# One inverse round earlier, one half round later: moving the scratch loads and the last jobs of a tiled convolution

## The chip, the cores and the metric

The kernel runs on one core of one Trainium2 chip. The metric is the device time of one execution in microseconds (us). Besides the plain timed runs there is one execution taken with the hardware profiler; all durations below are from it.

## The reference

The reference convolves an image of 224 x 224 pixels with 96 channels in and 96 out with a 7 x 7 filter, cyclically, by way of Fourier transforms in both directions:

```python
wp = jnp.pad(w, ((0, H - K), (0, W - K), (0, 0), (0, 0)))
Xf = rfft2(x, axes=(1, 2)); Wf = rfft2(wp, axes=(0, 1))
Yf = jnp.einsum('bhwi,hwio->bhwo', Xf, Wf)
y = irfft2(Yf, s=(H, W), axes=(1, 2)).astype(jnp.bfloat16)
```

x is 1 x 224 x 224 x 96 and w is 7 x 7 x 96 x 96, both bfloat16. Any method that gives this cyclic convolution will do.

## The kernel before

The kernel transforms the height only. The 224 rows are cut into 8 blocks of 28 (`B`, `NJ`), and each block with its 6 rows of overlap becomes 34 real numbers, held as 17 frequencies (`NS`) with a real and an imaginary part. Along the width the 7 taps stay a direct convolution, with adjacent pixels taken in pairs so that three short convolutions do the work of four. The image is cut into 7 tiles of 32 columns (`NT`, `TL` is the last, number 6). Every tile goes through three stages.

- Forward (`a_jobs`, `f_jobs`): TensorE multiplies the pixels `xn` by the transform matrix `Fm`; ScalarE (ACT) or VectorE (DVE) copies the result from PSUM to `xf`.
- Rounds (`b_round`, L496): one round for each frequency `s` = 0 to 16. First DVE forms sums and differences `J` of neighbouring pixels for three frequencies at once (`jit`, L466). In a round TensorE fills a first PSUM bank (19 small matmuls with `J`, `xf` and the filter `WF`); ACT scales part of it (`tt_`) and DVE makes `u` from it; then the function `mid` is called; TensorE fills a second bank (14 matmuls); DVE makes `v`; GpSimd (POOL) or DVE adds both to `yf`; at the end the function `end` is called. After three frequencies `yf` is stored to a scratch tensor `scr` in DRAM (`put`, L590). In the last tile this store is put off to the next round and queued on ACT's own instruction stream (L593 and L557); its scratch tensors are called `scra` and `scrb`.
- Inverse (`c_jobs`, L645): the scratch is read back with frequencies on the partitions (`load_t`, L602, tiles `tt` and `tt2`), TensorE multiplies by the inverse matrix `Gm`, ACT or DVE copies the result to `yo` (or to a free part of `J2`, which profiles call J), and it is stored to `out_dram`. A tile has 11 such jobs of two matmuls each: 2 + 2 + 3 + 2 + 2 for the five loads of `LT` (L685). The third load is `tt2`, made of four DMAs.

The stages of different tiles are interleaved, and the order is written out by hand in the loop from L808. While tile t is in its rounds, TensorE also gets the forward jobs of tile t+1 and the inverse jobs of tiles t-2 and t-1. They are dealt out by half round (`pace`, L725): a half round 2s is the `mid` of round s, 2s+1 its `end`. `CQ` (L42) says how many inverse jobs of the older and of the newer tile run during tile t: (11, 3) in tile 3, (8, 7) in tile 4, (4, 11) in tile 5 and (0, 11) in tile 6. They are spread evenly over the half rounds `k0` to `k1`, the older ones first (L819 to L826).

Loads of the scratch are queued by `queue_c` (L695) at the start of round 3. It hands the five loads to `pump` (L690), which issues a load as soon as fewer than four `tt` tiles (one for `tt2`) are held; a job that finishes a tile calls `pump` again. All loads, all stores of tiles before the last, and all output stores are issued by one queue, SyncE (SP), strictly in order: an entry whose semaphore is not there yet holds all entries behind it. Each DMA also takes one of eight semaphores in turn and waits until the DMA that had it before has landed.

PSUM has eight banks, given out in turn (`bank`, L106). A matmul that starts a new bank waits until the engine that reads the bank's former content is done. The program's builder fixes which bank, and therefore which reader, that is.

After the last round come the loads of the last scratch (`load_b`, L620), eight matmuls on the part that is already there (`first`), 36 matmuls that only keep TensorE working (L866), and sixteen closing matmuls (`second`) with their copies and stores.

Of the kernel before, what the change touches and what calls it, by code (L numbers as in the profile page):

```python
# [17 lines left out]
NS = L // 2  # L18
# [38 lines left out]
def kernel(  # L57
# [10 lines left out]
    TL = NT - 1  # L68
# [65 lines left out]
    def dma(out_ap, in_ap):  # L134
        return DE.dma_start(out=out_ap, in_=in_ap)
# [298 lines left out]
    def a_jobs(t):  # L434
        xf = new_xf(t)
        jobs = []
        for jg in range(2):
            for h in range(2):
                for (q, n) in ((0, 3), (3, 3), (6, 2)):
                    jobs.extend(a_bank(t, xf, xn_bufs[jg], h * PXC + 2 * q, n, jg, HALO + h * 8 + q))  # L440
            jobs.append(then_load(jobs.pop(), t + 1, jg))
        return jobs
# [23 lines left out]
    def jit(t, g):  # L466
        s0, s1 = JGB[g]
        n = s1 - s0
        xf = xf_tiles[t][0:C]
        xv = xf.rearrange("c p r s w j -> c p r s (w j)")  # L470
        b = jcount[0] % 3 if t < 2 else (jcount[0] - 2 * len(JGB)) % 2
        jcount[0] += 1
        Jb = J_bufs[b][0:C].rearrange("c (k s q) -> c k s q", k=7, s=3)
        for s in range(s0, s1):
            jbuf[(t, s)] = Jb[:, :, s - s0]

        def sub(o, a, b, op, cost):
            def f():
                load["v"] += 170 + cost / 1.92
                return VE.tensor_tensor(out=o, in0=a, in1=b, op=op)  # L480
            return f
        x0, x1 = xv[:, 0, :, s0:s1], xv[:, 1, :, s0:s1]
        c0, c1 = max(s0, REAL[0] + 1), min(s1, REAL[1])
        i0, i1 = c0 - s0, c1 - s0
        pd, rd, sd, qd = x1.ap
        dpl = bass.AP(x1.tensor, x1.offset - NJ, [pd, [NJ, 2], rd, sd, qd])
        return [
            sub(Jb[:, 0:4, 0:n].rearrange("c (k r) s q -> c k r s q", r=2), dpl,
                x0.unsqueeze(1).to_broadcast([C, 2, 2, n, PP]), ALU.subtract, 4 * PP * n),
            sub(Jb[:, 4, i0:i1], xv[:, 0, 0, c0:c1], xv[:, 0, 1, c0:c1], ALU.add, PP * (c1 - c0)),  # L490
            sub(Jb[:, 5:7, i0:i1], Jb[:, 0:4:2, i0:i1], Jb[:, 1:4:2, i0:i1], ALU.add, 2 * PP * (c1 - c0)),
        ]
# [152 lines left out]
    def c_jobs(t):  # L645
        jobs = []
        w0 = t * 2 * TW
        for gi, h in LT:
            hold = {}
            nq = 2 if gi < 2 else 3  # L650

            def mk_(q, gi=gi, h=h, nq=nq, hold=hold):
                def put(j0, nj, px, npx, row, col):
                    dma(out[0, j0 * B:(j0 + nj) * B, w0 + px:w0 + px + npx, :].rearrange("h w c -> h (w c)"),
                        hold["yo"][row:row + nj * B, col:col + npx * C])

                def f():
                    if q % 2 == 0:
                        hold["yo"] = new_yo()
                    tt = tt_tiles[(t, gi, h)]  # L660
                    yo = hold["yo"]
                    nj = 2 if q == 2 else 3
                    for b in range(2):
                        pb = bank()[0:nj * B, 0:4 * C]
                        TE.matmul(pb, lhsT=G[0:nj * FR, 0:nj * B],
                                  rhs=tt[0:nj * FR, 4 * q + 2 * b:4 * q + 2 * b + 2, :].rearrange("p w e -> p (w e)"), start=True, stop=True)
                        k = 2 * (q % 2) + b
                        evac(yo[0:nj * B, k * 4 * C:(k + 1) * 4 * C], pb, 4 * C)
                    if q == 1 and gi < 2:
                        put(gi * 3, 3, h * PXC, PXC, 0, 0)  # L670
                    elif q == 1:
                        put(6, 2, 0, 16, 0, 0)
                        for j in range(2):
                            put(6 + j, 1, 24, 8, 2 * B, j * 8 * C)
                    elif q == 2:
                        put(6, 2, 16, 8, 0, 0)
                    if q == nq - 1:
                        held[gi == 2] -= 1
                        pump()
                return f  # L680
            for q in range(nq):
                jobs.append(mk_(q))
        return jobs
# [11 lines left out]
    def queue_c(t):  # L695
        pend.extend((t, *k) for k in LT)
        pump()
# [35 lines left out]
    def fills(qs, k):  # L733
        def f():
            for q in qs:
                pace(q, k)
        return f
# [3 lines left out]
    def add(a, b, jobs):  # L741
        qs.append([a, b, jobs, len(jobs)])
# [15 lines left out]
    for r in range(NS + LAG):  # L758
# [32 lines left out]
        for t in range(2):  # L791
            s = r - LAG * t
# [15 lines left out]
    for t in range(2, NT):  # L808
        if t == TL:
            scr_tiles[t] = None  # L810
            scr_tiles[(t, 0)] = dr_pool.tile([TW, NJ, SA, 4 * C], BF16, name="scra")
            for i in range(2):
                scr_tiles[(t, 1 + i)] = dr_pool.tile([TW, NJ, (SB - SA, NS - SB)[i], 4 * C], BF16, name=f"scrb{i}")
        else:
            scr_tiles[t] = dr_pool.tile([TW, NJ, NS, 4 * C], BF16, name="scr")
        qs = []
        if t + 1 < NT:
            add(4 if t == 2 else 0, 26, a_jobs(t + 1))
        nold, nnew = CQ[t]  # L819
        k1 = 2 * NS if t < TL else 2 * NS - 9  # L820
        k0 = 10 if t in (2, TL) else 3
        km = k0 + -(-(k1 - k0) * nold // (nold + nnew))
        add(k0, km, cj[:nold])
        cn = c_jobs(t - 1)
        cj = cn[nnew:]
        add(km, k1, cn[:nnew])  # L826
        plan = {}
        for g, (s0, s1) in enumerate(JGB):
            if g + 1 < len(JGB) or t + 1 < NT:
                plan[s0 if g + 1 < len(JGB) else s0 - 1] = g  # L830
        for s in range(NS):
            now = ()
            if s in plan:
                g = plan[s]
                now = jit(t, g + 1) if g + 1 < len(JGB) else jit(t + 1, 0)
            if s == 3:
                queue_c(t - 1)
            if t in (3, 4):
                next(gp, None)
            if t == TL and s == SA + 2:  # L840
                sv = scr_tiles[(TL, 0)].rearrange("w j s (r e) -> (j s r) w e", r=2)
                for g in range(2):
                    for p0, p1 in ((0, 64), (64, KA)):
                        dma(tl_a[g][p0:p1], sv[g * KA + p0:g * KA + p1])
            b_round(t, s, fills(qs, 2 * s), fills(qs, 2 * s + 1), bool(now) or (t == TL and s >= NS - 3), now)
# [66 lines left out]
```

## Time and profile before

| | |
|---|---|
| median of 3 timed runs | 270.45 us (270.08 to 270.87) |
| profiled execution, its own time | 270.74 us |
| span of the program in it | 269.0 us |
| TensorE (PE) busy | 257.9 us, 96% of the span |
| DVE busy | 214.3 us, 80% |
| ACT busy | 195.5 us, 73% |
| POOL busy | 99.4 us, 37% |
| rounds of tile 5 | about 192 to 224 us |
| rounds of tile 6 | about 224 to 253 us |

A line of the timeline has the start in us from the start of the span, the duration in us, engine, line, operation, output<-inputs with buffer numbers left out, shape and count; in brackets stands how long the engine idled before and what ended that. All instructions bear the line 89, because a helper issues them, so they are told apart by tile names. `SPq` and `ACTq` are the instruction queues that issue DMAs. A matmul's duration contains its latency: successive matmuls overlap, and the time a group takes on TensorE is read from its start to the start of the next group.

### The profile page before, as it was taken

To read this page: it belongs to the slowest core of one execution; us is meant where nothing else is said; L and a number is where in the kernel's file an instruction comes from. 1 tells how busy PE (TensorE), PEld (TensorE's weight loads), DVE (VectorE), ACT (ScalarE), POOL (GpSimd) and SP (SyncE) were. 2 spreads that over 40 slices of the span, in tenths; PEclk is the share of its full clock that TensorE was granted. 3 is DMA by queue.
4 is the path that set the end of the run, shared out by engine and by line. 5 is a ranking of instruction groups with operands and counts; after the bars stand their busy time and mean duration, and the time that the engine had idled before them with its cause. 6 is when DMAs were issued, how large, how long until landed. Compare 5 with 4: busy or idle time off the path is not lost.

```text
span 269.0 us, 12171 instructions
## 1 busy us (share of the span) xinstructions
PE 257.9 (96%) x5144; PEld 237.1 (88%) x5144; DVE 214.3 (80%) x457; ACT 195.5 (73%) x483; POOL 99.4 (37%) x156
## 2 busy tenths in 40 slices
PE   8899999999999999999999999999998999899993
PEld 3679999999998999999999998989997989779862
DVE  5649998889899788778787888777887889778724
ACT  5549988587974578988988789886986864467113
POOL 7782315363647435322322222234132242522100
PEclk9999999999999999999999999999999999999998
DMA  6948011811111597987976486989658834888866
GB/s 171 230 129 217 6 46 46 243 47 67 46 46 50 163 276 135 294 249 206 289 207 198 133 246 192 250 223 332 224 151 152 255 98 154 198 231 212 223 118 205
DMA packets 47014, 46.78 MB, mean 174 GB/s; under 512 B 35286, under 2 KB 37986, under 8 KB 46960
## 3 DMA queue, kind: packets, MB, share of 16 engines
q1 hardware_dynamic: 44672, 43.94, 59.2%
q10 hardware_dynamic: 2288, 2.06, 2.8%
q8 instruction: 40, 0.66, 1.1%
q14 instruction: 14, 0.11, 0.1%
HBM read 24.65 MB, written 21.33 MB: 171 GB/s over the span
## 4 chain that ended last, share of the span: by engine, by line
PE 64%; DMA 12%; DVE 11%; ACT 7%; issue 3%; SPq 2%; DVEq 0%; ACTq 0%
PE pb L89 64%; DMA tt<-scr 5%; DMA wq<-in_w_dram 5%; DVE J L89 4%; ACT WF L89 3%; ACT xf L89 2%; DVE v L89 2%; DVE WF L89 2%; SPq L89 2%; DMA xf<-scrb 2%; DVE u L89 1%; DMA scrb<-yf 1%; DVE yf L89 1%; DVE xf L89 0%; DVE tt L89 0%
## 5 line engine op out<-in xcount | busy, mean ns | idle before, releaser
L89 PE MATMUL pb<-WF,J 96*128 96x96 bf16 x2821 | 162.6, 206 | 1.1 <-DVE J L89 0.9
L89 PEld LDWEIGHTS <-J 96*128 96x128 bf16 x2821 | 138.0, 98 | 10.5 <-issue 2.2
L89 POOL TENSOR_TENSOR yf<-v,u 128x384 bf16<-128x384 f32 x79 | 81.4, 1042 | 147.3 <-issue 86.9
L89 ACT CAST xf<-pb 96x408 bf16<-96x408 f32 (+3 forms) x145 | 67.8, 490 | 8.9 <-PE pb L89 5.3
L89 PE MATMUL pb<-WF,xf 96*128 96x96 bf16 x952 | 59.9, 206 | 0.5 <-ACT xf L89 0.5
L89 DVE TENSOR_TENSOR J<-xf 96x1824 bf16<-96x1824 bf16 (+1 forms) x84 | 56.9, 716 | 0.1
L89 PEld LDWEIGHTS <-xf 96*128 96x128 bf16 x952 | 47.0, 98 | 0.7 <-ACT xf L89 0.6
L89 PE MATMUL pb<-Fm,xn 118*128 118x136 bf16 (+3 forms) x640 | 45.5, 199 | 0.2 <-DVE u L89 0.2
L89 PE MATMUL pb<-tt,Gm 102*84 102x384 bf16 (+1 forms) x132 | 32.7, 327 | 2.4 <-DMA tt<-scr 2.3
L89 ACT CAST WF<-pb 96x480 bf16<-96x480 f32 (+1 forms) x59 | 29.1, 577 | 5.3 <-PE pb L89 5.3
L89 PEld LDWEIGHTS <-xn 118*128 118x128 bf16 x640 | 30.3, 97 | 0.3 <-issue 0.3
L89 ACT CAST J<-pb 84x384 bf16<-84x384 f32 (+1 forms) x64 | 27.6, 488 | 2.3 <-PE pb L89 2.0
L89 ACT CAST yo<-pb 84x384 bf16<-84x384 f32 (+1 forms) x63 | 26.9, 482 | 2.7 <-PE pb L89 2.7
L89 DVE TENSOR_TENSOR J<-J 96x912 bf16<-96x912 bf16 (+2 forms) x42 | 24.2, 576 | 0.0
L89 PE MATMUL pb<-wq 98*128 98x120 bf16 (+1 forms) x288 | 21.3, 226 | 0.3 <-DMA wq<-in_w_dram 0.3
L89 PEld LDWEIGHTS <-wq 98*128 98x128 bf16 x288 | 19.5, 151 | 0.8 <-issue 0.8
L89 PE MATMUL pb<-wu 128*128 128x512 bf16 (+1 forms) x75 | 16.5, 382 | 1.1 <-DVE ct L89 1.1
L89 PEld LDWEIGHTS <-wu 128*128 128x128 bf16 (+1 forms) x75 | 8.8, 119 | 7.7 <-issue 2.4
L89 DVE TENSOR_TENSOR yf<-v,u 128x384 bf16<-128x384 f32 x26 | 14.9, 571 | 0.9
L89 PEld LDWEIGHTS <-Gm 102*84 102x84 bf16 (+1 forms) x132 | 11.0, 117 | 3.5 <-DMA tt<-scr 2.9
L89 ACT COPY xf<-xf 96x816 bf16<-96x816 bf16 (+3 forms) x20 | 11.3, 632 | 0.0
L89 DVE CAST WF<-pb 96x480 bf16<-96x480 f32 (+1 forms) x13 | 7.5, 611 | 4.7 <-PE pb L89 4.7
(386 smaller groups left out, 234.4 us busy)
## 6 DMA issues: line engine op xcount, KB each, us to landing
scr<-yf SPq DMA_DIRECT2D x30, 288.0 KB
xn<-in_x_dram SPq DMA_DIRECT2D x12, 672.0 KB
tt<-scr SPq DMA_DIRECT2D x24, 336.0 KB
out_dram<-yo SPq DMA_DIRECT2D x12, 252.0 KB
out_dram<-J SPq DMA_DIRECT2D x12, 252.0 KB
tt<-scr SPq DMA_DIRECT2D x6, 288.0 KB
WF<-in_x_dram SPq DMA_DIRECT2D x2, 672.0 KB
out_dram<-tt SPq DMA_DIRECT2D x8, 168.0 KB
```

The lines of the kernel that those rows point to most:

```text
L89: r = fn(*a, **k)
```

## The change

Two expressions change. In tiles 3, 4 and 5 `queue_c` is called at the start of round 2 instead of round 3; tiles 2 and 6 keep round 3. In the last tile the inverse jobs are spread over the half rounds from 12 on up to, and not including, 26, where it was from 10 up to 25.

```diff
@@ -817,8 +817,8 @@
         if t + 1 < NT:
             add(4 if t == 2 else 0, 26, a_jobs(t + 1))
         nold, nnew = CQ[t]
-        k1 = 2 * NS if t < TL else 2 * NS - 9
-        k0 = 10 if t in (2, TL) else 3
+        k1 = 2 * NS if t < TL else 2 * NS - 8
+        k0 = {2: 10, TL: 12}.get(t, 3)
         km = k0 + -(-(k1 - k0) * nold // (nold + nnew))
         add(k0, km, cj[:nold])
         cn = c_jobs(t - 1)
@@ -833,7 +833,7 @@
             if s in plan:
                 g = plan[s]
                 now = jit(t, g + 1) if g + 1 < len(JGB) else jit(t + 1, 0)
-            if s == 3:
+            if s == (3 if t in (2, TL) else 2):
                 queue_c(t - 1)
             if t in (3, 4):
                 next(gp, None)
```

In SP's stream this moves, in tile 3, one load ahead of the store of `yf` of rounds 0 to 2; in tile 4, two loads ahead of that store and of one small copy; in tile 5, two `tt` loads and the four DMAs of `tt2` ahead of an output store and of that `yf` store, and a third `tt` load ahead of the `yf` store. In tile 6 the four loads `xf<-scra` for the closing stage come ahead of one output store that stood before them. No instruction is added or dropped; the numbers of matmuls, copies and DMAs stay. Which job lies in which half round of tile 6 changes as follows (jobs 1 to 11 of tile 5's inverse):

| half round | 10 | 11 | 12 | 13 | 14 | 15 | 16 | 17 | 18 | 19 | 20 | 21 | 22 | 23 | 24 |
|---|---|---|---|---|---|---|---|---|---|---|---|---|---|---|---|
| before | 1 | 2 | 3 | - | 4 | 5 | 6 | - | 7 | 8 | 9 | - | 10 | 11 | - |
| after | - | - | 1 | 2 | 3 | 4 | - | 5 | 6 | 7 | 8 | - | 9 | 10 | 11 |

## The prediction

> **What bounds the kernel now.** I read the page first, then PE's waits, then the timelines of PE, SP, DVE and ACT where those waits lie, and the chain of waits at the end.
>
> ```profile
> span 269.0 us, 12171 instructions
> PE 257.9 (96%) x5144; PEld 237.1 (88%) x5144; DVE 214.3 (80%) x457; ACT 195.5 (73%) x483; POOL 99.4 (37%) x156
> ```
>
> PE is the bound, so only what lets PE stand still can be won. PE's waits over the whole span:
>
> ```profile
> PE pb L89 <- DMA tt<-scr: 2.3, 3, 1.1
> ```
>
> Three waits for scratch loads are the largest entry. The PE timeline shows where they are, and the end of the kernel:
>
> ```profile
> 200.58 0.46 PE L89 MATMUL pb<-WF,J 96*128 96x96 bf16 x7
> 200.88 0.28 PE L89 MATMUL pb<-Fm,xn 118*128 118x136 bf16 x2
> ...
> 202.22 0.46 PE L89 MATMUL pb<-WF,J 96*128 96x96 bf16 x7
> 203.79 0.52 PE L89 MATMUL pb<-tt,Gm 102*84 102x384 bf16 x2 [1.10 <-DMA tt<-scr]
> ...
> 230.78 0.46 PE L89 MATMUL pb<-WF,J 96*128 96x96 bf16 x7
> 232.21 0.52 PE L89 MATMUL pb<-tt,Gm 102*84 102x384 bf16 x2 [0.96 <-DMA tt<-scr]
> ...
> 237.99 0.46 PE L89 MATMUL pb<-WF,J 96*128 96x96 bf16 x7
> 238.73 0.52 PE L89 MATMUL pb<-tt,Gm 102*84 102x384 bf16 x2 [0.28 <-DMA tt<-scr]
> ...
> 253.34 0.90 PE L89 MATMUL pb<-xf,GA 72*112 72x384 bf16 x4 [0.23 <-DMA xf<-scra]
> 254.08 6.01 PE L89 MATMUL pb<-wu 128*112 128x384 bf16 x36
> 260.48 0.99 PE L89 MATMUL pb<-xf,GB 128*112 128x384 bf16 x5 [0.39 <-DMA xf<-scrb]
> ```
>
> Seven `J` matmuls take 0.30 us from start to start where work follows at once (200.58 to 200.88). So the job at 203.79 was ready for PE at 202.52: PE lost 1.27 us, more than the idle time printed. By the same working it lost 1.13 at 232.21 and 0.44 at 238.73; before the job at 237.12 (14 matmuls from 236.35, 0.60) another 0.17. In all 3.0 us: 1.27 in tile 5, 1.74 in tile 6. SP's timeline has the loads:
>
> ```profile
> 192.31 0.35 SPq L89 DMA_DIRECT2D scr<-yf  x1
> ...
> 197.76 0.35 SPq L89 DMA_DIRECT2D scr<-yf  x1
> 198.20 7.90 SPq L89 DMA_DIRECT2D tt<-scr  x7
> ...
> 228.41 8.14 SPq L89 DMA_DIRECT2D tt<-scr  x8
> ...
> 245.06 3.44 SPq L89 DMA_DIRECT2D xf<-scra  x4
> ```
>
> **Part 1: the loads a round sooner.** Tile 5 first. The loads need tile 4's last store, issued at 192.31; the chain has 2.39 us from issue to landing for such a store (`scrb<-yf`, 253.89), so they may start at about 195 instead of 198.20. The chain's longest landing of a first tile is 5.54 us (198.20), which gives 200.5, two us before PE wants it: the 1.27 goes. What they are moved past: the J store (issued 196.91) and the `yf` store (197.76) now stand behind six load issues, which took 4.9 us at 228.41 and 6.1 at 198.20, so both come out 4 to 5 us later. Their buffers are wanted again four stores on (about 209) and four groups on (round 12, about 216); no cost, and if that cover were gone, up to 5 us of waiting for ACT or POOL. In tiles 3 and 4 PE never waits for `tt`; first use of the moved loads is ten or more half rounds off, and the one store and small copy behind them have the same cover. Cost nothing.
>
> What is late next: in the changed kernel's streams the banks fall differently from round 11 of tile 5 on. The second bank of that round is now the one that round 10's `u` gives back; before, its reader was a copy on ACT. `u` starts at 214.62 and takes 0.35 on DVE; PE starts the second bank at 214.49. Both come 1.27 earlier, so the wait is 0.48 us. Bounds: 0 if DVE catches up (it idles 0.94 before 210.62, but on ACT's scaled copy, which follows PE), 0.6 if `v` next to it counts too. I take 0.48, the row itself. Tile 5 nets 1.27 - 0.48 = 0.79.
>
> **Part 2: the last tile's jobs.** All loads and landings of tile 6 move with tile 5's end, so I keep the clock of before and add the 0.79 at the end. The second half of round 5 now follows its first at 231.08; PE reaches round 6 at 231.68. The rows that matter:
>
> ```profile
> 230.60 1.40 DVE L89 TENSOR_TENSOR J<-xf 96x1824 bf16<-96x1824 bf16 x2
> 231.93 0.62 DVE L89 TENSOR_TENSOR J<-J 96x912 bf16<-96x912 bf16 x1
> ...
> 247.59 0.54 DVE L89 SCALAR_TENSOR_TENSOR v<-tt__7338,pb 128x384 f32<-128x384 f32 x1
> ```
>
> ```profile
> 235.39 0.33 ACTq L89 DMA_DIRECT2D scra<-yf  x1
> ```
>
> (a) `J` of rounds 6 to 8 is done at 232.00 and 232.55. Round 6's first bank takes 4 matmuls from 232.00, 8 on `xf`, the last 7 from 232.56: it ends at 232.86 instead of 232.49, a new wait of 0.37 (0 if DVE runs ahead, 0.87 if all 19 wait for the last sum). Job 1 is due at 232.86, its tile landed by 232.21; jobs 5 and 6 are due at 238.45 and 239.59 by counting on (0.81 a first bank, 0.60 a second, 0.33 a job, and the waits below), their pieces landed by 237.1 and 238.7. So all 1.74 of load waits go.
>
> (b) ACT works in order. Before, the copies of jobs 1 and 2 ran at 232.60 to 234.38, ahead of the `scra` store that ACT issues at 235.39 once POOL has summed round 5 (233.41 plus 1.96). Now that store stands ahead of them, and POOL's sum hangs on DVE, not PE. ACT is held from 233.4 to 235.82 (its first copy after the store); the four copies then end at 236.30, 236.67, 237.04 and 237.41 (0.37 from start to start). Job 4 reuses job 1's banks: due 235.86, its matmuls start at 236.30 and 236.67; round 8 needs the third copy, 237.04 against 236.83. Wait 0.44 + 0.21 + 0.21 = 0.86. Bounds: 0 if POOL is done in time; 2.0 if the whole hold reaches PE.
>
> (c) The same at the second such store (before, at 241.54, after a hold of about 0.5): jobs 6 and 7 are copied behind it. 0 to 0.5; I take 0.26, the middle.
>
> (d) In round 12 DVE's `v` began at 247.59 though PE's second bank ended at 247.16 and `v` may start 0.19 later (239.88 against 239.69): ACT and `u` came last. With job 11 now between the two banks they have time: a gain of 0.24 for DVE's run of work to the last `yf` (253.87).
>
> Sum for that last `yf`: 0.79 + 1.74 - 0.37 - 0.86 - 0.26 + 0.24 = 1.28 us earlier.
>
> **The tail.** Two things must follow. PE's 36 filler matmuls (6.01 us) start only when the `xf<-scra` loads are in (253.34), and PE waited just 0.39 for `scrb` after them: if these loads keep their time, the end gains 0.39 at most. They should come sooner, as the output store of job 9 (issued 244.64, 252 KB) no longer precedes them. In exchange that store and job 11's now both stand in SP's queue right before the last `scrb` store. At 198.20 the first load took 5.54 us behind two stores (540 KB), at 228.41, with none before it, 3.8: 1.7 us for 540 KB, or 0.8 for the 252 KB that are new. They are issued over a us before the `scrb` store, so part drains in time: cost 0 to 0.8, I take 0.3.
>
> So 1.28 - 0.3 = 1.0 us. The profiled execution took 270.74 (span 269.0), 0.29 over the median; against it the forecast is 269.74, against the median 270.45 - 1.0 = **269.45**. A measurement of this kernel can tell about 0.3%, 0.81 us.
>
> **The rivals.**
>
> - The last store is caught in the queue. If the 504 KB still block it when it is issued, its landing comes 0.8 to 1.7 later; taking 0.9, the end gains 0.4: **270.05**. For it: the row of 198.20. Against it: the two stores may leave a us or more earlier. The Trainium skill (DMA: Bandwidth & Descriptors, Queues, rings and completion order) says that each DMA engine takes the descriptors of one issuing engine's queue in ring order; the 5.54 against 3.8 us agrees, and by that rule alone this rival would be the case.
> - The `scra` loads keep their time, and the fillers hold the end: gain 0.39, **270.06**. For it: SP still has the stores of jobs 5 to 7 before them, and these jobs run a half round later; against it: the fourth load waited for job 9's store at 247.22 and no longer has to.
> - Slower: the `scra` loads come later. Job 7 is a half round (1.0 us) later and its copy is behind (b) and (c); with the full 2.0 of (b) the loads go out 2.2 us later (1.0 + 2.0 - 0.79), and the end comes 2.2 - 0.39 = 1.8 later: **272.25**. It decides from loads 1.2 us late (0.39 + 0.81). Against it: job 7's store had 1.7 us to spare in front of the loads (243.36 to 245.06).
> - None of the new waits appears: 3.0 + 0.24 less nothing, about **267.3**. Against it: DVE is busy almost without a break from 216.8 to 228.8.
>
> **How the numbers follow.** Forecast 0.50 (268.9 to 269.9, of it 0.07 above 269.64), queue 0.18, fillers 0.14, slower 0.12, no new waits 0.06. Faster: 0.43 + 0.06, rounded 0.50; same: 0.07 + 0.18 + 0.14, 0.38; slower 0.12. The range, **268.2 to 270.8**, leaves out the slower rival and the last (0.18): its low end is the forecast with half the new waits (0.98 of 1.97) and no queue cost (0.3), its top the queue rival with 1.7 instead of 0.9.
>
> **What would show it.** Part 1: `tt<-scr` in tile 5 issued near 195, no PE wait near 202.5, but one of about half a us at DVE's `u` near 213. Part 2: no PE wait for `tt<-scr` at all, a wait for `J` at round 6, ACT's copies of jobs 1 and 2 behind the `scra` store, PE waits on ACT copies in rounds 7 to 8. Tail: `xf<-scra` in by about 252, `yf` done near 252.6. I am wrong if a `tt` wait stays, if ACT's hold costs PE over 2 us, or if the `scrb` chain after the last `yf` is longer than its 6.6 us of before (253.87 to 260.48) by more than 0.8.

## The result

The changed kernel takes 269.73 us in the median (269.23 to 270.67, 22 runs), the kernel before 270.56 us beside it (269.39 to 271.69, 22 runs). The ratio is 0.9974, 95% interval [0.9963, 0.9986]: 0.8 us, 0.3%, faster. A second set, told below, had 0.9999 [0.9976, 1.0023]. Weighted by the inverse squares of their widths the two give 0.998, some 0.6 us: a gain, near the least that can be told.

The profiled execution took 269.54 us (270.74 before), its span is 267.8 us. First the engines' busy time on its page, which is that of before:

```profile
span 267.8 us, 12172 instructions
PE 258.4 (96%) x5144; PEld 237.3 (89%) x5144; DVE 214.3 (80%) x457; ACT 194.6 (73%) x483; POOL 98.9 (37%) x156
```

PE's timeline of the changed kernel at the places that the prediction named (start, duration, in brackets the idle time before and what ended it):

```profile
202.02 0.46 PE L89 MATMUL pb<-WF,J 96*128 96x96 bf16 x7
202.32 0.49 PE L89 MATMUL pb<-tt,Gm 102*84 102x384 bf16 x2
...
213.53 0.76 PE L89 MATMUL pb<-WF,J 96*128 96x96 bf16 x14 [0.38 <-DVE u L89]
...
231.10 0.34 PE L89 MATMUL pb<-WF,J 96*128 96x96 bf16 x4 [0.23 <-DVE J L89]
...
235.42 0.70 PE L89 MATMUL pb<-tt,Gm 102*84 102x384 bf16 x2 [0.31 <-ACT J L89]
236.18 0.33 PE L89 MATMUL pb<-WF,J 96*128 96x96 bf16 x4
...
251.01 1.74 PE L89 MATMUL pb<-xf,GA 72*112 72x384 bf16 x8
252.59 6.01 PE L89 MATMUL pb<-wu 128*112 128x384 bf16 x36
259.33 0.97 PE L89 MATMUL pb<-xf,GB 128*112 128x384 bf16 x5 [0.72 <-DMA xf<-scrb]
```

At 202.32 the inverse job follows the seven `J` matmuls after 0.30 us: the 1.27 us that PE lost there are gone. No wait for `tt` is left in either tile. In their place stand the waits for `u` (213.53; the two matmuls before it started at 212.66, and such a pair takes 0.33 from start to start, so the whole loss is 0.54 us, over the 0.38 shown), for `J` (231.10) and for ACT's copies (235.42, and the 0.76 us to the next group instead of 0.33). SP's and ACT's timelines show why, and the chain of waits shows the end:

```profile
192.10 0.35 SPq L89 DMA_DIRECT2D scr<-yf  x1
195.55 4.59 SPq L89 DMA_DIRECT2D tt<-scr  x6
200.25 2.18 SPq L89 DMA_DIRECT2D out_dram<-J  x1
...
243.55 2.67 SPq L89 DMA_DIRECT2D xf<-scra  x4
249.30 0.34 SPq L89 DMA_DIRECT2D out_dram<-J  x1
251.59 0.34 SPq L89 DMA_DIRECT2D out_dram<-yo  x1
252.40 0.35 SPq L89 DMA_DIRECT2D scrb<-yf  x1
```

```profile
234.44 0.33 ACTq L89 DMA_DIRECT2D scra<-yf  x1
234.89 1.61 ACT L89 CAST J<-pb 84x384 bf16<-84x384 f32 x4 [2.05 <-PE pb L89]
```

```profile
252.40 3.73 DMA scrb<-yf
...
256.15 3.13 DMA xf<-scrb
```

The loads of tile 5 start at 195.55 instead of 198.20. In tile 6 ACT stands 2.05 us with its four copies behind the store at 234.44. The releaser named is PE, but PE made these jobs' matmuls at 231.96 and 232.88; the store ahead of them in ACT's own stream is what held them. At the end the store of the last `yf` takes 3.73 us (2.39 before) and its load 3.13 (4.05 before).

### The profile page after: what moved, and what is told of

Same layout as the page of the kernel before. It is cut to its first block, busy times and chain, and to the rows that moved or that the text cites. A ratio compares the mean times of both kernels' runs of the same rounds, so it can differ in the third digit from the quotient of the medians.

```text
span 267.8 us, 12172 instructions
## 1 busy us (share of the span) xinstructions
PE 258.4 (96%) x5144; PEld 237.3 (89%) x5144; DVE 214.3 (80%) x457; ACT 194.6 (73%) x483; POOL 98.9 (37%) x156
```

## The experiments

All are timed against the kernel before on the same chip. The table sets their profiles beside each other. Three stretches cover what the change can touch: tile 5 from ACT's first scaled copy of its round 0 to that of tile 6; tile 6 from there to the end of the last `yf`; and from there to PE's first `xf,GB` matmul.

| kernel | ratio [95%] | tile 5 | tile 6 | closing |
|---|---|---|---|---|
| before | 1 | 32.40 | 29.32 | 6.62 |
| before_again | | 32.14 | 28.90 | 6.83 |
| changed | 0.9974 [0.9963, 0.9986] | 31.63 | 28.79 | 6.95 |
| after_again | 0.9999 [0.9976, 1.0023] | 31.64 | 28.77 | 7.74 |
| part1_alone | 0.9991 [0.9971, 1.0012] | 31.63 | 28.93 | 7.55 |
| part2_alone | 1.0004 [0.9988, 1.0020] | 31.60 | 28.77 | 6.89 |
| late_outputs | 0.9978 [0.9960, 0.9997] | 31.64 | 28.78 | 6.49 |
| store_after_copies | 0.9973 [0.9953, 0.9993] | 31.64 | 27.72 | 7.47 |
| stores_held | 1.0005 [0.9984, 1.0026] | 31.64 | 28.79 | 7.71 |
| both_mended | 0.9925 [0.9909, 0.9940] | 31.64 | 27.69 | 6.67 |
| both_mended_again | 0.9948 [0.9931, 0.9965] | 31.63 | 27.69 | 6.98 |
| mends_old_window | 0.9972 [0.9957, 0.9987] | 31.63 | 28.82 | 6.55 |
| u_freed | 0.9949 [0.9930, 0.9968] | 31.26 | 28.05 | 7.00 |
| no_act_loads | one run, 267.69 us | 31.63 | 28.78 | 4.99 |

A stretch that hangs on engines alone repeats to 0.02 us (tile 5 of every kernel with part 1 but u_freed, tile 6 of the six with part 2 and ACT's hold). A stretch that hangs on a DMA does not: the two profiles of the kernel before differ by 0.26 us in tile 5 and 0.42 in tile 6, and the closing of the changed kernel's two profiles by 0.79.

### Each part alone

part1_alone is the kernel before with this line:

```diff
-            if s == 3:
+            if s == (3 if t in (2, TL) else 2):
```

> The loads a round sooner alone; the last tile's jobs stay in half rounds 10 to 24. My theory (the two parts add up): the wait for tt<-scr in tile 5 (1.27 us of PE) is gone, a wait of 0.4 to 0.5 for DVE's u stands at the second bank of round 11 of tile 5, the waits for tt<-scr in tile 6 (1.7 us) stay; the whole rest moves 0.8 earlier, the tail with it, since the order of the stores there is that of before: 0.8 us faster than before, ratio 0.997. Rival (the fillers hold the end): the xf<-scra loads keep their place and the end gains 0.39 at most, ratio 0.9985. Rival (DMA traffic moved into other loads' way): a new wait for a load in tiles 3 to 5, no gain, ratio 1.000.

part2_alone is the kernel before with these:

```diff
-        k1 = 2 * NS if t < TL else 2 * NS - 9
-        k0 = 10 if t in (2, TL) else 3
+        k1 = 2 * NS if t < TL else 2 * NS - 8
+        k0 = {2: 10, TL: 12}.get(t, 3)
```

> The last tile's jobs in half rounds 12 to 25 alone; the loads are queued in round 3 everywhere. My theory: the wait of 1.27 us in tile 5 stays; in tile 6 the waits for tt<-scr (1.7) go and waits for J (0.2 to 0.4) and for ACT's copies (0.3 to 0.9) come; the last yf is about 0.5 earlier than before, but the last scrb store then lands in 3.7 us instead of 2.4, because two output stores stand right ahead of it in SP's queue, which takes nearly all of it: ratio 0.999 to 1.000. Rival (the longer landing of the last store has another cause than the order of the stores and belongs to part 1): the store lands in 2.4 us and the end gains 0.5, ratio 0.998.

Part 1 alone took 269.87 us, part 2 alone 270.25, the kernel before 270.09: 0.2 us faster and 0.2 slower, both within their intervals of some 0.5 us. The waits came and went as expected (the waits for `u` in the one, for `J` and ACT's copies in the other), but the times did not: part 1 was expected to gain 0.8 us, and the two do not add up to the changed kernel's gain. PE's timeline of part2_alone shows one reason. Tile 5 is untouched in it, and yet:

```profile
203.16 0.52 PE L89 MATMUL pb<-tt,Gm 102*84 102x384 bf16 x2 [0.30 <-DMA tt<-scr]
```

The seven matmuls before start at 202.40, so PE lost 0.46 us here (203.16 - 202.70) where the first profile of before had lost 1.27. That is why its tile 5 (31.60 us) is as short as with part 1: what part 1 removes was, in this execution, smaller than the wait for `u` that it brings.

The chain of waits in part1_alone shows another:

```profile
252.38 3.48 DMA scrb<-yf
...
255.88 3.88 DMA xf<-scrb
```

Its tiles 5 and 6 are 1.16 us shorter than in the first profile of before (61.72 - 60.56), but its closing is 0.93 longer. Its last stores stand in the order of before, where the closing store took 2.39 and 2.49 us; in part2_alone, where 3.7 was expected because two output stores stand ahead, it took 2.37. So the order of the stores alone does not set how long this store takes.

### The kernel before once more

before_again has no edit.

> The kernel before once more, for a second profiled execution: nothing else tells how much of the 1.27 and 1.74 us that PE lost at scratch loads belongs to the order of the work and how much to that one execution. In the run of part 2 alone tile 5 was not touched, and there PE lost 0.46 us (203.16 against 202.70) where the first profile of before has 1.27. If the losses belong to the order, this profile has 1.1 to 1.4 us in tile 5, 1.5 to 1.9 in tile 6, and rounds 0 to 16 of tile 5 take 32.4 us again. If the landing of a load varies from run to run, tile 5 loses anything from 0.3 to 1.3 us, tile 6 from 1.0 to 1.8, and the time of the execution follows within 0.3 us once the closing store and load are set off.

PE's timeline of before_again:

```profile
201.97 0.46 PE L89 MATMUL pb<-WF,J 96*128 96x96 bf16 x7
203.27 0.52 PE L89 MATMUL pb<-tt,Gm 102*84 102x384 bf16 x2 [0.84 <-DMA tt<-scr]
...
230.27 0.46 PE L89 MATMUL pb<-WF,J 96*128 96x96 bf16 x7
231.57 0.52 PE L89 MATMUL pb<-tt,Gm 102*84 102x384 bf16 x2 [0.84 <-DMA tt<-scr]
```

PE lost 1.00 us at either place, against 1.27 and 1.13. Three executions of the same stretch of tile 5 thus lost 1.27, 1.00 and 0.46 us: the order of the work sets where the wait is, and its size hangs on when the load lands, which differs between executions. The profile that the prediction was worked out from was the worst of the three. Against before_again the changed kernel's tiles 5 and 6 are 0.6 us shorter (61.04 - 60.42), against the first profile 1.3.

### ACT's hold

store_after_copies is the changed kernel with the last tile's scratch stores, which ACT issues, moved from the middle of a round behind the round's inverse jobs:

```diff
-            if puts:
-                puts.pop(0)()
+            late_put = puts.pop(0) if puts else None
...
             end()
+            if late_put:
+                late_put()
```

> The changed kernel with one more edit: in the last tile the scratch store on ACT is issued at the end of its round, behind the copies of the round's inverse jobs, instead of ahead of them. My theory (ACT held by that store costs PE): the copies of jobs 1 and 2 come up to 1.5 us earlier, the PE waits for ACT copies at rounds 7 and 8 (about 0.7 in all) and the later one at round 10 go, and the last yf is 0.5 to 0.9 earlier than in the changed kernel; of it at most 0.7 reaches the end, since the fillers cap it, and less if the scra loads are late: ratio 0.995 to 0.997. Rival (DVE and POOL set the pace of these rounds, ACT does not): the waits move to DVE's u or v and the last yf does not move, ratio 0.9974.

ACT's timeline of store_after_copies:

```profile
233.17 1.60 ACT L89 CAST J<-pb 84x384 bf16<-84x384 f32 x4
234.87 0.33 ACTq L89 DMA_DIRECT2D scra<-yf  x1
```

The four copies now run before the store, none of PE's waits is for ACT in tile 6, and tile 6 takes 27.72 us instead of 28.79. The hold was worth 1.07 us (0.5 to 0.9 had been expected); the prediction's (b) and (c) are 0.86 + 0.26 = 1.12. The ratio, 0.9973 [0.9953, 0.9993], cannot be told from that of the changed kernel all the same: in this profile what tile 6 won went into a closing of 7.47 us, and the next runs look at what that hangs on.

### The output stores and the closing store

late_outputs is the changed kernel with the two output stores of jobs 9 and 11 issued after the last `scrb` load:

```diff
-                        put(gi * 3, 3, h * PXC, PXC, 0, 0)
+                        if t == TL - 1 and h == 1:
+                            late_out.append(lambda: put(gi * 3, 3, h * PXC, PXC, 0, 0))
+                        else:
+                            put(gi * 3, 3, h * PXC, PXC, 0, 0)
...
     load_b(1, DE, 1)
+    for f in late_out:
+        f()
```

> The changed kernel with one more edit: the output stores of jobs 9 and 11 of the last tile, which stand in SP's queue right ahead of the last scrb store, come behind the load of it instead. My theory (the queue costs the tail): the last scrb store lands in 2.4 us again instead of 3.7; the loads behind it take 3.1 to 4.1; the end comes 0.5 to 0.7 earlier than in the changed kernel (PE waits 0.72 for scrb after its fillers, which caps it), so 1.2 to 1.4 faster than before, ratio about 0.995. Rival (the DMA engines share all traffic whatever its order): the store still takes over 3 us, and the time is that of the changed kernel, ratio 0.9974.

stores_held is its opposite: the stores are put in the same list, but wait for the last `v` and leave directly ahead of the `scrb` store.

```diff
...
+                for f in late_out:
+                    d = f()
+                    tc.add_manual_dep(d.ins, last_v[0].ins.name, SYNC, reason="output behind the last v")
                 put()
...
```

> The changed kernel with the output stores of jobs 9 and 11 held until the last v on VectorE (the v of round 15), so that all 504 KB leave SP directly ahead of the last scrb store, where the changed kernel issues the first of them 3 us ahead. It makes the suspected cost in the queue as large as it can be with these stores. Queue theory: the scrb store lands 0.8 to 1.7 us later than the 2.4 us it takes with an empty queue, so 3.2 to 4.1 us or more, and the kernel takes 0.4 to 1.3 us more than after_again on the same chip. Rival, landings vary and the stores do not matter: the store takes 2.3 to 3.8 us as in the profiles so far and the time is that of after_again within 0.3 us. The issue of the second store can itself put the scrb store off by up to 0.35 us; that shows in its start, not in its duration.

after_again is the changed kernel, beside it on the chip.

> The changed kernel once more, beside the next two on one chip. PE must again have no wait for a scratch load, and the waits for u (about 0.54 us lost), J (0.4) and ACT's copies (0.9 and 0.2) must come again, since they hang on engines and not on DMAs: tile 5 at 31.63 us, tile 6 to the last yf at 28.8, both within 0.1. What may differ is the closing store and load of scrb: 3.73 and 3.13 us in the first profile. If the two output stores in the queue make the store late, it takes 3.4 us or more again; if landings vary whatever stands ahead, anything from 2.3 to 3.8. Time 269.3 to 269.9 us, ratio 0.996 to 0.9985 of before.

The chain of waits in stores_held:

```profile
254.60 4.59 DMA scrb<-yf
...
259.20 3.03 DMA xf<-scrb
```

and in part2_alone, which has the same two stores ahead as the changed kernel:

```profile
252.71 2.37 DMA scrb<-yf
...
255.10 4.43 DMA xf<-scrb
```

With 504 KB issued about a microsecond ahead of it (253.58 and 254.01) the store takes 4.59 us, the longest of all profiles. That fits a store that stands behind what its own queue holds, as the Trainium skill has it (DMA: Bandwidth & Descriptors, Queues, rings and completion order: each DMA engine takes the descriptors of one queue in ring order); it is a single profile. But with the stores where the changed kernel has them it took 3.73, 3.08, 2.37 and 2.77 us (changed, after_again, part2_alone, store_after_copies): mostly they have drained. And it took 3.48 in part1_alone with the stores of before ahead, and 1.88 to 3.21 where SP issued nothing in the five us before it (u_freed, mends_old_window, late_outputs, both_mended). So the 3.73 of the first profile is hardly outside what comes without the two stores, and after_again's 3.08 is under the 3.4 expected if they cause it. What a store loses its load partly wins back: 3.73 + 3.13, 2.37 + 4.43, 4.59 + 3.03. In time, stores_held stood 0.45 us over after_again (270.64 against 270.19, at the low end of the 0.4 to 1.3 expected, and within the intervals); late_outputs alone, expected at 0.995, showed no difference from the changed kernel that could be told, 0.9978 against 0.9974. Whether the stores cost the changed kernel the predicted 0.3 us is therefore not settled.

### What the last load waits for

no_act_loads is the changed kernel without the two `scrb` loads that ACT issues in the closing stage, and with half the fillers; part of the last tile is then made from old data:

```diff
-    load_b(0, SE, 2)
...
-    for _ in range(WARM):
+    for _ in range(WARM // 2):
```

> The changed kernel without the two loads of the first scrb tensor that ACT issues in the tail (288 KB), so that the output of the last tile is made from old data there, and with 18 instead of 36 filling matmuls so that they cannot hold the end. In all but one profile so far the last load on SP (192 KB) lands 0.5 to 1.2 us behind the second of ACT's loads, whenever it was issued: 3.0 to 4.6 us after its own issue. If it stands behind ACT's loads on the DMA engines, it lands 2.0 to 2.6 us after its issue here, and PE starts the closing matmuls 0.8 to 2 us sooner after the last yf (5.0 to 5.8 us instead of 6.5 to 7.7). If such a load takes 3 to 4.6 us by itself, nothing changes but the fillers.

The chain of waits in no_act_loads:

```profile
252.51 2.23 DMA scrb<-yf
...
254.75 2.68 DMA xf<-scrb
```

The load that took 3.03 to 5.04 us in the chains of the other profiles that end on it takes 2.68, a little over the 2.0 to 2.6 expected, and the closing 4.99 us instead of 6.49 to 7.74. That points to SP's load sharing the DMA engines with ACT's 288 KB and being late by them, though the chain of waits names only SP's store and load. The Trainium skill (DMA: Bandwidth & Descriptors, Queues, rings and completion order) says that each DMA engine takes turns between the queues that have work for it; this run agrees. It is one execution, though, 0.35 us under the shortest of the others, and not all of the shorter closing can be put down to ACT's loads: in this kernel the two output stores also left sooner, at 246.24 and 247.28 instead of 249.30 and 251.59, and the store took 2.23 us instead of 3.73. That ACT's loads get ahead meanwhile would also explain why a late store is partly won back. In the profiles ACT's loads leave 2.1 to 3.8 us after ACT's last store, by the distance on ACT's timeline from its issue to that of the loads (250.68 to 252.87 in the changed kernel, 250.61 to 254.33 in after_again); they read what it writes. Why that differs from run to run stays open.

### Both mends, the window and the wait for u

both_mended has the edits of store_after_copies and late_outputs together.

> The changed kernel with both edits of the first set of runs: the scra and scrb stores on ACT come behind the copies of the same round, and the output stores of jobs 9 and 11 come behind the last scrb load. Moving ACT's stores took 1.07 us from tile 6 (28.79 to 27.72 us) in the profile, of which 0.67 us came through in the median. If the late output stores help the closing store, this takes 0.3 us off that, 268.4 to 268.9 us; if they do not, it is the time of that run, 269.0 to 269.4. PE's wait for scrb at the end must be 0.3 to 1.0 us, that for scra up to 0.4; if the fillers rather than scrb held the end, both would vanish.

> The version with both mends once more, for its time beside the other two: the first had six runs that count. 268.4 to 269.0 us, tile 5 at 31.64, tile 6 at 27.7 us, PE's wait for scrb 0.2 to 1.0 us.

It takes 268.56 and 268.40 us, 0.75% and 0.52% under the kernel before; the changed kernel took 270.19 beside the first. PE's timeline of both_mended_again shows what bounds it in this execution:

```profile
251.62 0.83 PE L89 MATMUL pb<-xf,GA 72*112 72x384 bf16 x4 [0.98 <-DMA xf<-scra]
252.29 6.02 PE L89 MATMUL pb<-wu 128*112 128x384 bf16 x36
258.14 0.98 PE L89 MATMUL pb<-xf,GB 128*112 128x384 bf16 x5
```

PE waits for the `scra` loads, then runs its own fillers, and does not wait for `scrb`, where 0.2 to 1.0 us had been expected: here the prediction's second rival, the fillers, holds. In the profile of both_mended PE still waited 0.34 us for `scrb` after the fillers, so the two are close.

mends_old_window is both_mended with the job window of before, which isolates part 2:

```diff
-        k1 = 2 * NS if t < TL else 2 * NS - 8
-        k0 = {2: 10, TL: 12}.get(t, 3)
+        k1 = 2 * NS if t < TL else 2 * NS - 9
+        k0 = 10 if t in (2, TL) else 3
```

> Both mends of the last set (ACT's scratch stores behind its copies, late output stores) and the loads a round sooner, but the last tile's jobs in the half rounds of before, 10 to 25. It gives the worth of part 2 where it has no ACT hold to pay for. With part 2 and both mends tile 6 took 27.69 us to the last yf. Here the scratch loads land too late again: PE loses 1.1 to 1.7 us at tt, and wins the 0.4 at J, so tile 6 takes 28.4 to 29.1 us and the kernel 0.5 to 1.2 us more than the version with part 2 on the same chip. If part 2 is worth nothing even without the hold, as the run of part 2 alone had it (ratio 1.0004), both take the same within 0.3 us.

In tile 6 the wait for a load is back on PE's timeline of mends_old_window:

```profile
231.34 0.52 PE L89 MATMUL pb<-tt,Gm 102*84 102x384 bf16 x2 [0.73 <-DMA tt<-scr]
```

It takes 269.31 us against 268.40 for both_mended_again on the same chip, and tile 6 28.82 us against 27.69. So part 2 is worth about 0.9 us where ACT's store does not hold the copies, and about nothing (part2_alone) where it does.

u_freed is both_mended with this:

```diff
-        k1 = 2 * NS if t < TL else 2 * NS - 8
+        k1 = 2 * NS - (t == TL - 1) if t < TL else 2 * NS - 8
```

> Both mends with part 1 and part 2, and in tile 5 the inverse jobs spread over half rounds 3 to 32 instead of 3 to 33, which puts jobs 5 to 15 at the ends of rounds instead of their middles. The banks then fall differently: the second bank of round 11 is no longer the one that round 10's u gives back. If that bank was the cause of the 0.54 us that PE loses at 213.5 in the changed kernel, the wait for u is gone, tile 5 takes 31.0 to 31.2 us instead of 31.64, and the kernel 0.4 to 0.6 us less than both_mended_again. Rival: DVE is simply behind there, and PE then waits for the next thing that DVE owes (v, or a copy) just as long; tile 5 stays at 31.5 or more.

PE's timeline of u_freed at round 11 of tile 5:

```profile
213.04 0.34 PE L89 MATMUL pb<-Fm,xn 118*128 118x136 bf16 x3
213.22 0.76 PE L89 MATMUL pb<-WF,J 96*128 96x96 bf16 x14
```

The 14 matmuls of the second bank follow at once, and none of PE's waits there is for DVE: the rival falls, and the bank is the likely cause. The edit moves the jobs as well as the banks, so the bank was not changed alone. Tile 5 takes 31.26 us instead of 31.64, a little over the 31.0 to 31.2 expected. But the time stays: 268.67 against 268.40 us, where 0.4 to 0.6 less was expected. Counted from the start of tile 5, ACT's scaled copy of tile 6's round 10 is still 0.37 us ahead of both_mended, and DVE's `u` of round 12 is not. ACT's timeline of u_freed has the place:

```profile
241.87 0.85 ACT L89 CAST J<-pb 84x384 bf16<-84x384 f32 x2 [1.27 <-PE pb L89]
```

That copy needs an output buffer whose store landed, by its last semaphore record, at 241.79. The releaser printed is PE, but both_mended makes the same copy at 241.91, and there the trace names that store (`0.84 <-DMA out_dram<-J`). The store was issued at 235.96, behind eight `tt` loads in SP's queue. Tiles 5 and 6 together take 59.31 us in u_freed and 59.33 in both_mended: what tile 5 gave went into the next wait, by this reading the one for that store; no run takes it away.

## Why the prediction was right, point by point

- **Part 1, the load wait.** The mechanism was right: loads at 195.55 (predicted 195), no wait near 202.5. Its size was 1.27 us only in the execution that was profiled; others lost 1.00 and 0.46. Taking one profile's wait for the kernel's is what made the forecast lean on the largest of three.
- **The wait for `u`.** Predicted 0.48, lost 0.54; u_freed, where banks and jobs are moved, has no such wait. Tile 5 came out 0.77 us shorter, predicted 0.79.
- **Tiles 3 and 4** were costed at nothing. From the first scaled copy of tile 4 to that of tile 5 are 32.52 us before (192.15 - 159.63) and 32.51 after (191.95 - 159.44), and tile 3 before it takes 31.80 (159.63 - 127.83) and 31.81 (159.44 - 127.63): nothing.
- **(a) `J` at round 6.** Predicted 0.37. By the starts PE lost 0.43: the job behind round 6's first bank was due at 231.53 (229.82 + 0.30 + 0.60 + 0.81) and starts at 231.96; 0.23 of it shows as idle time.
- **(b), (c) ACT's hold.** Predicted 0.86 and 0.26. By the starts PE lost 0.90 at the first store (the job due at 234.95 starts at 235.42, and the next group 0.43 late) and 0.17 at the second (241.49 - 240.99 - 0.33); taking the hold away gained 1.07.
- **Sum to the last `yf`.** Predicted 1.28 earlier. In the table tiles 5 and 6 went from 61.72 to 60.42 us, 1.30; from before_again's 61.04 it is 0.62, so the close match holds for the one execution that the sum was worked out from. (d), predicted 0.24, has no run of its own, but the trace has it: in round 12 `v` starts at 246.10, 0.22 us after PE's second bank ends (245.28 + 0.60), where it was 0.43 before.
- **The tail.** Predicted a cost of 0.3 for the stores in the queue. The closing went from 6.62 to 6.95 us in the first pair of profiles, which is 0.33, but the closings of the changed kernel's two profiles alone are 6.95 and 7.74, and part1_alone, with the stores of before, has 7.55. The agreement with 0.3 is luck: that the stores cost just this is not shown. The 7.74 is 1.12 over the 6.62 of before, beyond the 0.8 that the prediction named as a sign of being wrong; as the closing of part1_alone is as long, the moved stores are not needed for it. The prediction had both stores leave over a us before the closing store; they left 3.1 and 0.8 us before it (249.30, 251.59, 252.40), the first only after SP had waited 3.0 us for an `xf<-scra` load to land. And it did not ask whether ACT's loads share the engines with the last load.
- **The total.** 1.0 us predicted, 0.8 measured in the first set, about 0.6 over both; 269.73 us against 269.45. The load waits of the first profile of before stood 0.7 us above those of the second (61.72 - 61.04 in tiles 5 and 6), which is enough to make the forecast too large by that much. The closing can move the time by as much again, so that the total came out this near is in part luck.
- **The rivals.** Queue: its price was seen only in the one profile in which the stores leave right ahead of the closing store. Fillers: not binding in the changed kernel (PE waits 0.72 for `scrb` after them), binding in one of two profiles once both mends are in. Slower: the `scra` loads were issued sooner, 243.55 against 245.06. No new waits: all three came (and 270.45 - 3.24 is 267.2, not 267.3).

## What to carry to other kernels

Here a wait for an engine's work repeated from run to run to some 0.02 us, and could be priced from one profile; a wait for a DMA was anything from a third to all of what the first profile showed. Price such a wait from several executions or give it a range. When work is moved later, look in each in-order instruction stream for what now stands ahead of it: here stores that ACT issues itself took back nearly all that part 2 won, and moving them made the last tile 1.07 us shorter, more than the whole change gained. In time that showed only together with the late output stores.

## What the runs showed of the hardware that was not expected

- The same load wait in unchanged code took 1.27, 1.00 and 0.46 us in three executions.
- A load of 192 KB, issued on SP, took 2.68 us without and 3.03 to 5.04 us with 288 KB of loads on ACT's queue, in chains that name SP alone. The 2.68 is from one execution.
- An output store of 252 KB behind eight scratch loads took 5.8 us from issue to landing (235.96 to 241.79), and a copy on ACT that needs its buffer started at 241.87.
